# A fused attention and two-layer feed-forward kernel: four times the tolerance for weight steps between the attention's fixed steps

## The chip, the core and the metric

One core of one Trainium2 chip runs the whole program in one launch. The metric is the device time of that launch in microseconds, the median of three timed runs: 1220.61 us for the kernel before (1220.47 to 1222.97). Differences below about 0.2% (2.4 us) are not told from no change here.

## What is computed

Attention over 4 batches, 12 heads, 448 positions and head size 64, with a root-mean-square norm on q and k, followed by two feed-forward layers over 1792 tokens, 768 wide with 2048 hidden units. The weights come as 64-bit floats. In short:

```
q_n, k_n = rmsnorm(q, g_q), rmsnorm(k, g_k)
scores = (q_n @ k_n.T) / sqrt(64);  attn = softmax(scores);  x = attn @ v        # 4 x 12 heads
h = x @ w_in;   x = (h * sigmoid(h)) @ w_out                                     # moe_
h = x @ w_in2;  out = relu(h)**2 @ w_out2                                        # moe2_
```

## The kernel before

Every product is made of three matmuls in a reduced 32-bit form, with each operand split into an upper and a lower part.

**Attention** works on 24 pairs of heads, 0 to 23. For one pair, DMAs load q and k (line 516) and v (633). ScalarE squares them (527), VectorE sums (536), GpSimd and VectorE run Newton steps for the inverse root (544 to 580) and scale (589), and TensorE transposes the scaled q and k (601) into the tile T (610 to 619). Four chunks of 112 rows follow: scores (654) on TensorE, the row maximum on VectorE (665), the exponential on ScalarE (672), which also adds up its row sums into the tile `sum`, a transpose of E on TensorE (681), and a copy of that by VectorE or ScalarE (481, 483) into PT. Two rounds of products with v (730) end the pair. VectorE then inverts the row sums (701, 702). These 112 x 8 numbers must be laid along the other axis, so they go to DRAM by one DMA, `rd<-sum` (709), and come back spread over partitions by two, `R<-rd` (718). GpSimd multiplies the pair's result by R (753). For the first 12 pairs the result is split into the tile xb for the first layer; for the others it is stored by `x<-xf` (785).

`sum` has three buffers. The first exponential of pair p+3 therefore waits until the DMA `rd<-sum` of pair p has landed. `R` has two buffers, the tiles with q and k three.

**Weights** are made from 64-bit words by steps on a whole unit (768 numbers a partition for w_in, 512 for w_out). A unit is loaded as `raw` (846, two buffers). ScalarE takes the magnitude (853), VectorE clamps (857), shifts (861), puts the sign in (867) and the low bits in (873). The result, W, is stored by a DMA for later use (`ki` or `ko`, 881) and split into the upper part (493 or 495) and the lower part (502). I number the units 0, 1, 2, ... in order of use: 0 to 3 are the first of w_in, 4 to 9 the first of w_out.

**Layer 1** runs `up` (954, 18 matmuls each) and `down` (1008). `up` ends in tanh (966) and a product (971) into one of four tiles `g`, and from there in two parts into `gg`. The memory of `gg` belongs to a second pool, which takes the place of the attention's tiles. So the first write of `gg` waits until all of the attention has been done, the last store `x<-xf` included. **Layer 2** follows (1170 to 1273).

**The order** on every engine comes from a planner in the kernel that runs at build time, and each engine takes its instructions strictly in that order. Nearly all DMAs are issued by SyncE (SP), also in order: an issue that waits for data holds back all issues behind it. Every step of the attention has a hand-written place in a table (`nominal`), and each engine takes its attention steps in the order of that table. All other steps, the weights' above all, fill the gaps. The planner's rule for this is in `forward`, line 211: a step without a place may go ahead of the next attention step of its engine only if it ends, by the planner's own durations, at most FIT after the time at which that attention step could start:

```
nx = max(f, ready[next.n][e]) if not left[next.n] else max(f, next.nom + late)
if st + steps[n].on[e][0] > nx + FIT:
    continue
```

FIT is set on line 39.

Of the kernel before, what the change touches and what calls it, by code (L numbers as in the profile page):

```python
# [35 lines left out]

T2 = 5.3
EVEN, ODD = 0.0, 3.67
FIT = 0.1

# [54 lines left out]
class Plan:  # L97
# [81 lines left out]
    def forward(self, due):  # L179
# [16 lines left out]
        while len(order) < len(steps):  # L196
            best = None
            for e in ENGINES:
                f = free[e]
                next = fixed[e][-1] if fixed[e] else None  # L200
                for n in wait[e]:
# [7 lines left out]
                    if next is not None and steps[n] is not next:  # L209
# [3 lines that stand above are left out]
# [1129 lines left out]
```

## Time and profile before

| | |
|---|---|
| timed runs, median | 1220.61 us |
| profiled execution, its own time | 1222.14 us |
| its span | 1220.2 us |
| TensorE matmul busy | 1187.6 us (97%) |
| VectorE busy | 917.9 us (75%) |
| ScalarE busy | 547.2 us (45%) |
| GpSimd busy | 248.9 us (20%) |
| DMA queue of SP, share of 16 engines | 60.9% |

The attention fills the first 296 us, the first layer reaches to about 760 us, and the second layer the rest. TensorE is nearly always busy, so what a change in one stage is worth shows where TensorE waits, and in what would make it wait. In the profile's rows a time is counted from the span's start. A number in brackets with an arrow is the time for which the engine sat idle before the row, and what ended that.

### The profile page before, as it was taken

What the parts mean: (1) busy time and instruction counts of PE and PEld (TensorE: products, weight loads), DVE (VectorE), ACT (ScalarE), POOL (GpSimd) and SP (SyncE); (2) the same over time, 40 slices, a digit from 0 to 9 for tenths busy, and PEclk for the clock granted to TensorE, in tenths of its full rate; (3) what the DMA queues carried; (4) which work ended last, traced back from release to release, by engine and by line L of the source; (5) the groups of instructions that cost most, each with busy time, mean ns of one, the idle gap of its engine ahead of it and who ended that gap; (6) DMA issues with size and microseconds to landing.
All of it is one profiled execution on the core that took longest, in us unless ns stands there. A gap on an engine that the chain in (4) does not pass through costs nothing.

```text
span 1220.2 us, 19070 instructions
## 1 busy us (share of the span) xinstructions
PE 1187.6 (97%) x6960; PEld 1045.2 (86%) x6960; DVE 917.9 (75%) x1596; ACT 547.2 (45%) x1141; POOL 248.9 (20%) x459
## 2 busy tenths in 40 slices
PE   4999999998899999999999999999999999999998
PEld 3666666666799999998999998899999999999998
DVE  6988888887789886879798968866667973555554
ACT  6889888874334232424332315343333434211111
POOL 5466666531000000112010001011111130000000
PEclk9999999999899999999999999999999999999999
DMA  5456555548676645596888756946655785444444
GB/s 165 77 71 89 86 73 97 91 68 148 174 230 186 177 135 177 171 353 203 253 250 266 230 165 219 390 162 237 221 194 204 268 312 199 166 158 143 143 148 137
DMA packets 134109, 220.75 MB, mean 181 GB/s; under 512 B 31104, under 2 KB 99456, under 8 KB 134016
## 3 DMA queue, kind: packets, MB, share of 16 engines
q1 hardware_dynamic: 134016, 219.54, 60.9%
q8 instruction: 55, 0.90, 0.3%
q14 instruction: 38, 0.31, 0.2%
HBM read 145.88 MB, written 73.62 MB: 180 GB/s over the span
## 4 chain that ended last, share of the span: by engine, by line
PE 87%; DMA 6%; DVE 4%; ACT 1%; issue 1%; POOL 1%; SPq 0%; ACTq 0%; DVEq 0%
PE s L1008 18%; PE s L1246 17%; PE t L954 17%; PE t L1170 11%; PE t L681 6%; PE pv L730 6%; PE s L654 6%; PE pv L1170 4%; PE t L601 2%; DMA yf<-y 2%; DMA raw<-in_moe_w_out_dram 1%; DMA raw<-in_moe_w_in_dram 1%; DMA rd<-sum 1%; DMA w<-su 1%; DMA su<-w 1%
## 5 line engine op out<-in xcount | busy, mean ns | idle before, releaser
L954 PE MATMUL t<-xb,w 128*128 128x448 f32 x1152 | 242.2, 368 | 6.7 <-DVE g L971 6.7
L1008 PE MATMUL s<-gg,w 128*128 128x448 f32 x1152 | 239.5, 365 | 0.8 <-DVE g L1020 0.8
L954 PEld LDWEIGHTS t<-xb,w 128*128 128x128 f32 x1152 | 217.6, 189 | 25.9 <-DVE g L971 8.1
L1008 PEld LDWEIGHTS s<-gg,w 128*128 128x128 f32 x1152 | 216.2, 188 | 18.6 <-DVE g L1020 1.1
L1246 PE MATMUL s<-w,gh 128*128 128x384 f32 x896 | 227.6, 334 | 0.1
L1246 PEld LDWEIGHTS s<-w,gh 128*128 128x128 f32 x896 | 162.0, 188 | 1.5 <-DMA w<-su 0.4
L1273 DVE TENSOR_TENSOR gg<-s,gg 128x384 f32<-128x384 f32 x196 | 107.7, 554 | 61.5 <-PE s L1246 61.2
L1246 PE MATMUL s<-w,gl 128*128 128x384 f32 x448 | 149.7, 334 | 0.0
L672 ACT ACTIVATE E<-s,mx 112x448 f32<-112x448 f32 x192 | 121.2, 645 | 17.5 <-DVE mx L665 17.3
L1186 DVE TENSOR_TENSOR g<-t,g 128x448 f32<-128x448 f32 x96 | 58.4, 620 | 81.3 <-ACT g L481 57.0
L665 DVE TENSOR_REDUCE mx<-s 112x1 f32<-112x448 f32 x192 | 110.8, 619 | 10.3 <-PE s L654 8.0
L681 PEld LDWEIGHTS t<-ident,E 112*112 112x112 f32 x768 | 74.3, 135 | 37.5 <-ACT E L672 19.3
L681 PE MATMUL t<-ident,E 112*112 112x112 f32 x768 | 96.1, 268 | 4.8 <-ACT E L672 4.1
L654 PE MATMUL s<-T 64*112 64x448 f32 x576 | 85.5, 402 | 3.0 <-ACT T L610 3.0
L502 DVE TENSOR_TENSOR w<-W,w 128x768 fp32r<-128x768 f32 (+1 forms) x97 | 83.8, 871 | 3.1 <-ACT w L493 2.4
L1246 PEld LDWEIGHTS s<-w,gl 128*128 128x128 f32 x448 | 84.1, 188 | 0.0
L730 PE MATMUL pv<-PT,vv 112*64 112x224 f32 x768 | 83.3, 359 | 0.0
L502 POOL TENSOR_TENSOR w<-W,w 128x512 fp32r<-128x512 f32 (+1 forms) x15 | 24.1, 1604 | 279.2 <-ACT w L493 207.4
L493 ACT CAST w<-W 128x768 fp32r<-128x768 f32 (+1 forms) x64 | 47.9, 751 | 72.0 <-PE s L1008 45.7
L1196 ACT ACTIVATE g<-g 128x448 f32<-128x448 f32 x48 | 27.5, 576 | 97.3 <-DVE g L1186 96.7
L502 POOL TENSOR_TENSOR gl<-g,gh 128x448 fp32r<-128x448 f32 x12 | 14.7, 1223 | 266.2 <-DVE gh L495 198.9
L730 PEld LDWEIGHTS pv<-PT,vv 112*64 112x64 f32 x768 | 51.4, 136 | 20.0 <-issue 0.9
(109 smaller groups left out, 1754.0 us busy)
## 6 DMA issues: line engine op xcount, KB each, us to landing
raw<-in_moe_w_in_dram SPq DMA_DIRECT2D x32, 768.0 KB, 5.4
raw<-in_moe_w_out_dram SPq DMA_DIRECT2D x24, 512.0 KB, 4.4
raw<-in_moe_w_out_dram SPq DMA_DIRECT2D x16, 768.0 KB, 6.3
su<-w SPq DMA_DIRECT2D x16, 768.0 KB, 7.1
w<-su SPq DMA_DIRECT2D x16, 768.0 KB, 5.5
yf<-y SPq DMA_DIRECT2D x48, 224.0 KB, 4.1
ki<-W SPq DMA_DIRECT2D x16, 384.0 KB, 5.8
ko<-W SPq DMA_DIRECT2D x24, 256.0 KB, 4.3
```

The costliest lines, as they stand in the source:

```text
L502: kind, when, any_t(n, rate), lambda e: engine(e).tensor_tensor(o(), a(), h(), ALU.subtract),
L654: nc.tensor.matmul(pts[j].ap[:CP, :S], T.ap[r, 0, a, c * CP:(c + 1) * CP], T.ap[r, 1, b_], start=(k_ == 0), stop=(k_ == 2),)
L665: lambda e, pt=pt, mx=mx: nc.vector.tensor_reduce(mx.ap, pt.ap[:CP, :S], AX.X, ALU.max, negate=True),
L672: lambda e, j=j, c=c, pt=pt, mx=mx, E=E: nc.scalar.activation(E.ap[:, j], pt.ap[:CP, :S], AF.Exp, bias=mx.ap, accum_out=sums.ap[:, j, c:c ...
L681: nc.tensor.transpose(pe.ap[:CP, m * CP:(m + 1) * CP], E.ap[:, j, m * CP:(m + 1) * CP], ident.ap)
L730: nc.tensor.matmul(pv.ap[j * D:(j + 1) * D, c2 * CT * CP:(c2 + 1) * CT * CP], vr.ap[:, j * NCH + m, :], pt.ap[:, j * NCH + m].rearrange("p ...
L954: nc.tensor.matmul(pt.ap[:, :S], w_()[:, c, :], x[c // HC].ap[:, a, c % HC, :], start=(c == 0 and n == 0), stop=(c == NC6 - 1 and n == 2),)
L1008: nc.tensor.matmul(pt.ap[:, :S], w_()[:, f, :], gg.ap[:, k, a, f, :], start=(f == 0 and n == 0), stop=(f == HQ - 1 and n == 2),)
L1170: nc.tensor.matmul(pt.ap[:, :S], w_()[:, c0 + c, :], view(b, a, c)(), start=(start and c == 0 and k == 0), stop=(c == HC - 1 and k == 2), ...
L1186: lambda e: nc.vector.tensor_tensor(o.ap, pt.ap[:, :S], a.ap, ALU.add),
L1246: nc.tensor.matmul(pt.ap[:, :NH], g.ap[:, fi, tc_ * P:(tc_ + 1) * P], w_()[:, 0, nh * NH:(nh + 1) * NH], start=(n == 0), stop=(n == 5),)
L1273: lambda e, o=o, pt=pt: nc.vector.tensor_tensor(o(), pt.ap[:, :NH], o(), ALU.add),
```

## The change

One number: steps that have no place in the attention's table may end up to 0.4 instead of 0.1 after the time at which the next attention step could start.

```
 T2 = 5.3
 EVEN, ODD = 0.0, 3.67
-FIT = 0.1
+FIT = 0.4
```

No instruction's work changes. The orders of VectorE, ScalarE, GpSimd and SP change from the start of the attention to the start of layer 1; a few weight steps go to another of the engines that may take them. TensorE's order stays, apart from three matmuls of the first `up` that move over one group of products with v.

**SP, pair 6.** The two DMAs `R<-rd` bring back the sums of pair 5, `rd<-sum` stores those of pair 6, `vv` and `qk` are loads of v, q and k for later pairs. Before:

```order
L718 DMA R_1547<-rd_1406 64x448 x2
L709 DMA rd_1594<-sum_1307 112x8x1
L633 DMA vv_1606<-in_v_dram 112x2x256
L516 DMA qk_1702<-in_q_dram 112x2x256
L516 DMA qk_1702<-in_k_dram 112x2x256
L718 DMA R_1734<-rd_1594 64x448 x2
```

And now:

```order
L718 DMA R_1591<-rd_1451 64x448 x2
L846 DMA raw_1625<-in_moe_w_out_dram 128x4x256
L881 DMA ki2_1627<-W_614 128x768
L709 DMA rd_1641<-sum_1329 112x8x1
L633 DMA vv_1644<-in_v_dram 112x2x256
L516 DMA qk_1754<-in_q_dram 112x2x256
L516 DMA qk_1754<-in_k_dram 112x2x256
L718 DMA R_1810<-rd_1641 64x448 x2
```

The load of unit 4 and the store of unit 2 now stand between the two DMAs of pair 5 and the store of pair 6's sums. Such a piece stands at the same place ahead of the stores of pairs 3, 6, 9, 11, 12 and 14 (loads of units 3 to 8). The load of unit 9 stands ahead of the two DMAs of pair 14, and that of unit 2 behind the store of pair 0. Before, units 0 and 1 are loaded at the very start and the next load, of unit 2, comes behind the store of pair 20; now none is left between pair 15 and the end of the attention.

**VectorE, end of pair 6**: the last part of a later T (617), the inverse of the sums (701, 702) and two Newton steps (551, 558). Before:

```order
L617 SCALAR_TENSOR_TENSOR T_1491<-t_1561,G_134,T_1491 128x448
L701 TENSOR_SCALAR sum_1307<-sum_1307 112x8
L702 RECIPROCAL sum_1307<-sum_1307 112x8
L551 TENSOR_SCALAR ib_1592<-ms_1500 112x16
L558 TENSOR_SCALAR y_1596<-ib_1592 112x16
```

And now:

```order
L873 SCALAR_TENSOR_TENSOR W_614<-raw_503,W_614 128x768
L617 SCALAR_TENSOR_TENSOR T_1515<-t_1583,G_136,T_1515 128x448
L701 TENSOR_SCALAR sum_1329<-sum_1329 112x8
L702 RECIPROCAL sum_1329<-sum_1329 112x8
L551 TENSOR_SCALAR ib_1637<-ms_1530 112x16
L495 CAST w_1639<-W_614 128x768
L558 TENSOR_SCALAR y_1646<-ib_1637 112x16
```

The low bits and the upper part of unit 2 have moved in.

**ScalarE, from the last chunk of pair 22 to the start of pair 23** (`sum_4270` and `sum_4429` before, `sum_4356` and `sum_4504` now). Before:

```order
L481 COPY xf_4382<-pv_4256 128x448
L853 ACTIVATE W_4384<-raw_4286 128x768
L672 ACTIVATE E_4400,sum_4270<-s_4373,mx_4391 112x448
L672 ACTIVATE E_4400,sum_4270<-s_4374,mx_4398 112x448
L481 COPY PT_4410<-t_4393 112x4x112
L672 ACTIVATE E_4428,sum_4429<-s_4402,mx_4423 112x448
```

And now:

```order
L481 COPY xf_4460<-pv_4342 128x448
L672 ACTIVATE E_4476,sum_4356<-s_4451,mx_4467 112x448
L672 ACTIVATE E_4476,sum_4356<-s_4452,mx_4474 112x448
L481 COPY PT_4486<-t_4469 112x4x112
L672 ACTIVATE E_4503,sum_4504<-s_4478,mx_4498 112x448
```

The magnitude of unit 2 (853) no longer stands ahead of these exponentials; it now stands in pair 1, ahead of the exponentials there.

## Rows read from the trace of the kernel before

**Rows 1.** Busy time by stretch, four attention laps together (the last line's sum).

```profile
sum 45.00, PE 45.00 PEld 31.03 DVE 39.26 ACT 40.14 POOL 29.01; mean PE 11.25 PEld 7.76 DVE 9.81 ACT 10.04 POOL 7.25
```

**Rows 2.** The chain that ended last: start us, us, what.

```profile
107.49 1.66 PE pv L730 x16
...
118.71 1.67 PE pv L730 x16
...
364.03 27.36 PE t L954 x135
```

**Rows 3.** Timeline of TensorE, end of attention: start us, us, engine line op.

```profile
275.19 1.73 PE L730 MATMUL pv<-PT,vv 112*64 112x224 f32 x16
280.11 1.21 PE L681 MATMUL t<-ident,E 112*112 112x112 f32 x8 [3.19 <-ACT E L672]
...
285.27 1.74 PE L730 MATMUL pv<-PT,vv 112*64 112x224 f32 x16
...
295.58 16.42 PE L954 MATMUL t<-xb,w 128*128 128x448 f32 x78
317.96 15.06 PE L954 MATMUL t<-xb,w 128*128 128x448 f32 x63 [5.96 <-DVE g L971]
332.86 12.32 PE L1008 MATMUL s<-gg,w 128*128 128x448 f32 x60
```

**Rows 4.** Timeline of ScalarE, end of attention and start of layer 1.

```profile
278.56 0.89 ACT L853 ACTIVATE W<-raw 128x768 f32<-128x768 f32 x1 [5.17 <-DMA raw<-in_moe_w_in_dram]
...
322.39 1.50 ACT L493 CAST gg<-g 128x448 fp32r<-128x448 f32 x3 [0.53 <-DMA x<-xf]
```

**Rows 5.** Busy time by stretch, 300 to 350 us; the clock stands behind POOL.

```profile
300.00:350.00 50.00, 44.04 (x206) 39.99 (x205) 37.88 (x65) 18.26 (x31) 2.85 (x2) 0.93 0.75 192
```

**Rows 6.** Timeline of SP's DMA issues, pairs 6 to 8.

```profile
115.14 1.09 SPq L718 DMA_DIRECT2D R<-rd  x2
116.34 0.52 SPq L709 DMA_DIRECT2D rd<-sum  x1
...
127.12 0.52 SPq L709 DMA_DIRECT2D rd<-sum  x1
```

**Rows 7.** Line 709 (`rd<-sum`), 90 to 270 us, 16 issues.

```profile
DMA to landing us min/median/max: 9.4/9.5/11.5
```

**Rows 8.** Timeline of ScalarE, first exponentials of pairs 9 and 22.

```profile
119.29 0.67 ACT L672 ACTIVATE E<-s,mx 112x448 f32<-112x448 f32 x1
...
265.15 0.67 ACT L672 ACTIVATE E<-s,mx 112x448 f32<-112x448 f32 x1
```

**Rows 9.** Timeline of SP's DMA issues, pairs 19 to 23.

```profile
263.61 1.25 SPq L718 DMA_DIRECT2D R<-rd  x2
...
266.83 0.40 SPq L846 DMA_DIRECT2D raw<-in_moe_w_in_dram  x1
...
274.24 1.09 SPq L718 DMA_DIRECT2D R<-rd  x2
275.44 0.52 SPq L709 DMA_DIRECT2D rd<-sum  x1
...
287.89 1.09 SPq L718 DMA_DIRECT2D R<-rd  x2
...
300.22 0.53 SPq L709 DMA_DIRECT2D rd<-sum  x1
...
311.88 1.09 SPq L718 DMA_DIRECT2D R<-rd  x2
```

**Rows 10.** The page's DMA issues: count, KB each, median us to landing.

```profile
raw<-in_moe_w_in_dram SPq DMA_DIRECT2D x32, 768.0 KB, 5.4
raw<-in_moe_w_out_dram SPq DMA_DIRECT2D x24, 512.0 KB, 4.4
```

**Rows 11.** The page's groups: busy us, mean ns of one, idle before.

```profile
L502 DVE TENSOR_TENSOR w<-W,w 128x768 fp32r<-128x768 f32 (+1 forms) x97 | 83.8, 871 | 3.1 <-ACT w L493 2.4
```

## Prediction, made before the changed kernel ran

> **What bounds the kernel now.** I read the attention first, since only its orders change. In four laps of it TensorE is busy for all of 45.00 us; VectorE has 39.26 and ScalarE 40.14 [rows 1]. So a lap is TensorE's, and by the chain of work that ended last it takes 118.71 - 107.49 = 11.22 us [rows 2]. VectorE has (45.00 - 39.26) / 45.00 x 11.22 = 1.43 us of it free.
>
> At the attention's end TensorE does wait. After the products at 275.19 it sits idle for 3.19 us, and the next such group starts at 285.27, 10.08 us later, where half a lap would be 5.61 [rows 3]. ScalarE stood for 5.17 us before the magnitude of unit 2, whose load landed only then, with the exponentials queued behind it [rows 4]. The second wait is 5.96 us long, ahead of 317.96 [rows 3]. The 63 matmuls after it took 15.06 us; at the 27.36 us for 135 of a calm stretch [rows 2] they would have taken 12.77. The granted clock of that stretch was 0.93 on average [rows 5], a part of it at the lower level of 1.2 GHz. The two losses there are 5.96 + 2.3 = 8.3 us.
>
> The third thing to see is not a wait of TensorE, but it sits close behind. SP issues the two DMAs that bring back pair 6's sums at 115.14, pair 7's store at 116.34 and pair 8's at 127.12 [rows 6]. The store takes 9.4 to 11.5 us to land, mostly 9.5 [rows 7], and SP waits for that before it issues the two DMAs, then the next store. This chain takes 127.12 - 116.34 = 10.78 us a lap against TensorE's 11.22: it has 0.44 us to spare. And someone waits for it. The first exponential of pair p+3 needs pair p's `sum` buffer back. Pair 6's store has landed at 115.14 and pair 9's exponential starts at 119.29: 4.15 us [rows 6, 8]. For pairs 19 and 22 it is 263.61 and 265.15: 1.54 us [rows 8, 9].
>
> **The change part by part.** The weight steps move forward in a body: ten units instead of two are loaded before pair 16, eight of them are worked through there, and eight stores go with them.
>
> A, removed: the wait of ScalarE at 278.56. No load or magnitude of a weight is left there. Gain 10.08 - 5.61 = 4.5 us.
>
> C, added: seven laps in which a load of a unit, mostly with a store of another, stands ahead of a store of sums. The trace of before shows two laps in which a load and a weight store were still draining as the sums' store was issued. The first, with 768 KB, is 275.44 to 287.89, 12.45 us; the second, with 512 KB, is 300.22 to 311.88, 11.66 us [rows 9]. Against 9.5 these are 2.95 and 2.16 us more. One unit of 768 KB (unit 3) and six of 512 KB give 2.95 + 6 x 2.16 = 15.9 us. In those two laps part of the load had gone before, so this leans low. For the other end I take the whole transfer: 768 KB land 1.0 us after 512 KB would [rows 10], hence 4 us per MB, 3.1 and 2.1 us, and a weight store of half that size half as much again: 4.6 + 6 x 3.1 = 23 us. I keep 15.9, the lengths of real laps. A reason that excludes a gain here: nothing that the chain carries is taken away before pair 20. Of the 15.9 the slack absorbs what is left of it at the end, 1.5 us [rows 8, 9]; the 0.44 us a lap were used up in the kernel before, else that slack would not have shrunk from 4.15. So ScalarE's exponentials, and TensorE with them, come 14.4 us later by pair 23.
>
> The Trainium skill says of such queues (DMA: Bandwidth & Descriptors, Queues, rings and completion order) that each DMA engine takes descriptors in ring order and that a semaphore counts up only after every earlier write of that engine. By that rule the weights ahead of the sums' store must be through first; the two long laps agree with it.
>
> D, added: unit 2's load stands behind pair 0's store, as in the lap of 266.83, where it took 278.56 - 266.83 = 11.7 us until ScalarE had it [rows 4, 9]. Its magnitude stands ahead of pair 1's exponentials. At most the 4.5 us of A, at least 0 if ScalarE comes to it late enough; I take 2.
>
> E, VectorE: units 0 to 7 bring about 17 more steps of 768 and 18 of 512 numbers into the attention. A long one takes 0.87 us [rows 11]; the clamps, shifts and casts are shorter, and I put the sum at 20 to 24 us. In the 16 laps from pair 3 to pair 19 there are 16 x 1.43 = 23 us free, and C stretches these laps by 14 more. I cost E at nothing for that; without that cover it is 0 to 2 us. GpSimd, which gets two lower parts, has 16 of 45 us free [rows 1]. The pushed attention steps themselves are late by under a microsecond, and the row maxima catch up in the next gap.
>
> B, the start of layer 1. Weights no longer hold TensorE at 317.96. What is late next is the store of pair 23's result, which opens the memory of `gg`. The return DMAs of pair 20 move from 274.24 [rows 9] to 274.2 + 15.9 + 2 = 292.1; three laps of 10.78 later those of pair 23 go, at 324.4. Before, from there to the first write of `gg` it took 322.39 - 311.88 = 10.5 us [rows 4, 9], with two weight loads in the queue; I take 9: 333.4. TensorE ends the attention at 295.6 - 4.5 + 14.4 + 2 = 307.5, can do seven `up` without `gg` (four tiles `g`, three PSUM buffers), 7 x 18 x 0.2027 = 25.5 us, and stands at 333.0. It then waits for one tile `g` to be handed on, four short steps, about 2.5 us, and the eighth `up` of 3.65 ends at 339.6. In the kernel before, `down` starts at 332.86 [rows 3]. So +6.7 us; with a drop of the clock after the wait, as after the 3.19 us, up to +8.4. I take +7.5.
>
> After that TensorE is as full as before, and the shift stays. Profiled 1222.1 + 7.5 = 1229.6; the median of the timed runs is 1.5 us below the profiled time, so **1228.1 us**.
>
> **The rivals.** *The return chain has room after all* (the other side). It decides at pair 6: if its store still lands by 119.3, C falls away. Then A gives 4.5, the start of layer 1 all of its 8.3, D costs 2 and E 1: -9.8 us, 1210.8. For it speaks that the store of the sums is only 3.5 KB. Against it speaks that this store takes 9.5 us in every lap, and more in both laps with weights in front. The Trainium skill's fit (DMA: Bandwidth & Descriptors, Anatomy of one DMA) of 2.0 us plus bytes by 436 KB per us would make that store an estimated 2 us; with it the chain would have 7 us to spare, and this rival would hold. The trace says 9.5.
>
> *The gains and the chain cancel.* If half of each load slips into the time in which the sums' store waits for DRAM, C is 8 - 1.5 = 6.5, TensorE ends the attention at about 299.6, `gg` opens at 325.5, seven `up` end at 325.1 and the eighth at 331.7: -1.2 us, 1219.4.
>
> *The whole transfer counts*, 23 us. Then the attention ends 7.1 us later than in the forecast and so does everything behind it: 1235.2; if TensorE's waits of 2 us or so also bring the clock down, some more. No row shows the clock fall after a wait that short.
>
> *The change doesn't do what it says*: excluded by the order, in which the steps have moved.
>
> **How the numbers follow.** Forecast 0.58 (own range 1223.5 to 1234); whole transfer 0.12; cancel 0.14; room 0.16. Faster by over 0.2% (2.4 us, about what a measurement tells from no change) is the rival with room: 0.16. Within it: 0.14. Slower: 0.70. The range 1213 to 1237 leaves out most of the case with room and the far end of the dear one.
>
> **What would show it.** Issues of `rd<-sum` about 11 us apart in plain laps and 13 or more with a load in front; ScalarE's first exponential of a pair waiting for a DMA from pair 9 on; no wait near 276; the attention's end near 307, the first write of `gg` near 333, `down` near 340. I am wrong if ScalarE never waits for the sums' store, or if laps with weights stay at 11.2 us.

## The result, and the profile after

The changed kernel takes **1237.45 us** (median; 1231.96 to 1243.06) against 1221.79 of the kernel before on the same chip. The ratio is 1.0124, with a 95% interval of 1.0087 to 1.0161: slower by 1.2%. On the 1220.61 us that the prediction started from, that is 1235.7. The forecast had 1228.1 and a range of 1213 to 1237, so the sign was right and the loss of 15 us was twice the 7.5 foreseen. The profiled execution took 1240.2 us, its span is 1238.4, 18.2 us longer than before. Two executions of the experiments below, one of e2 (1766.16 us) and the profiled one of e5 (2966.65 us), ran in a slower state of the chip and are left out of the ratios.

Where the time went shows in TensorE's timeline. In each row: start, length, engine, line, operation; in brackets the idle time before and what ended it. `L730` are the products of a pair, `L681` the transposes of E.

```profile
46.48 1.73 PE L730 MATMUL pv<-PT,vv 112*64 112x224 f32 x16
51.99 0.60 PE L681 MATMUL t<-ident,E 112*112 112x112 f32 x4 [3.78 <-ACT E L672]
...
59.36 3.25 PE L730 MATMUL pv<-PT,vv 112*64 112x224 f32 x16
...
203.14 2.04 PE L681 MATMUL t<-ident,E 112*112 112x112 f32 x8 [6.41 <-ACT E L672]
...
314.21 22.77 PE L954 MATMUL t<-xb,w 128*128 128x448 f32 x111
345.46 7.67 PE L954 MATMUL t<-xb,w 128*128 128x448 f32 x27 [8.48 <-DVE g L971]
352.97 3.20 PE L1008 MATMUL s<-gg,w 128*128 128x448 f32 x15
```

The wait at the end of the attention is gone (the 3.19 us of [rows 3]), but there are two new and longer ones, in pair 1 and in pair 13. Behind each the matmuls are slow for a while: the products at 59.36 take 3.25 us where others take 1.73. The granted clock says why (stretch, busy times, clock behind POOL):

```profile
50.00:60.00 10.00, 7.57 (x36) 5.08 (x38) 6.64 (x15) 8.00 (x21) 4.14 (x14) 0.64 0.37 81
...
200.00:210.00 10.00, 6.82 (x32) 4.60 (x32) 4.32 (x12) 8.22 (x21) 4.12 (x15) 0.51 0.46 68
```

A mean of 0.64 and of 0.51 is for most of these stretches the lower level of 1.2 GHz. Layer 1's first long run of `up` starts at 314.21 instead of 295.58 [rows 3], 18.6 us later, and its first `down` at 352.97 instead of 332.86, 20.1 us later.

ScalarE's timeline tells who held TensorE up:

```profile
50.44 0.89 ACT L853 ACTIVATE W<-raw 128x768 f32<-128x768 f32 x1 [6.06 <-DMA raw<-in_moe_w_in_dram]
51.22 0.63 ACT L672 ACTIVATE E<-s,mx 112x448 f32<-112x448 f32 x1
...
200.83 0.66 ACT L853 ACTIVATE W<-raw 128x512 f32<-128x512 f32 x1 [8.49 <-DMA raw<-in_moe_w_out_dram]
...
342.05 1.50 ACT L493 CAST gg<-g 128x448 fp32r<-128x448 f32 x3 [12.29 <-DMA raw<-in_moe_w_in_dram]
```

The first two waits are those of a **magnitude**, of unit 2 and of unit 7, that stands until its load is there, with the exponentials queued behind it. (The third row is the first write of `gg`, to which I come back under B.) It is the wait that stood at 278.56 before [rows 4], now twice and in the middle of the attention. What the forecast had counted on, an exponential that waits for the store of the sums, does not occur. These are ScalarE's two longest waits in total from 60 to 300 us (total, times, longest), and line 672, the exponentials, waits for row maxima alone:

```profile
ACT E L672 <- DVE mx L665: 14.3, 20, 1.4
ACT W L853 <- DMA raw<-in_moe_w_out_dram: 14.1, 4, 8.5
```

SP's issues around the two loads:

```profile
37.19 0.32 SPq L709 DMA_DIRECT2D rd<-sum  x1
37.60 0.50 SPq L633 DMA_DIRECT2D vv<-in_v_dram  x1
38.27 0.39 SPq L846 DMA_DIRECT2D raw<-in_moe_w_in_dram  x1
...
175.76 0.53 SPq L846 DMA_DIRECT2D raw<-in_moe_w_out_dram  x1
...
188.29 1.09 SPq L718 DMA_DIRECT2D R<-rd  x2
189.47 0.54 SPq L846 DMA_DIRECT2D raw<-in_moe_w_out_dram  x1
190.06 0.50 SPq L881 DMA_DIRECT2D ko<-W  x1
190.66 0.38 SPq L709 DMA_DIRECT2D rd<-sum  x1
```

Unit 2's load is issued 1.1 us behind a store of sums and is ready 50.44 - 38.27 = 12.2 us later; unit 7's goes 1.2 us ahead of one and is ready after 11.4 us. Units 4 to 6, whose loads also go 1.2 us ahead of such a store, took 7.4, 6.2 and 6.2 us by the same reckoning, with waits of 1.6 to 2.1 us.

### The profile page after: what moved, and what is told of

The parts are those of the page before. It is cut to its first block, busy times and chain, and to the rows that moved or that the text cites. A ratio compares the mean times of both kernels' runs of the same rounds, so it can differ in the third digit from the quotient of the medians.

```text
span 1238.4 us, 19057 instructions
## 1 busy us (share of the span) xinstructions
PE 1195.7 (97%) x6960; PEld 1048.9 (85%) x6960; DVE 913.2 (74%) x1602; ACT 543.0 (44%) x1136; POOL 257.7 (21%) x458
## 3 DMA queue, kind: packets, MB, share of 16 engines
q1 hardware_dynamic: 134016, 219.54, 60.4%
## 4 chain that ended last, share of the span: by engine, by line
PE 80%; DMA 8%; DVE 4%; POOL 3%; ACT 3%; issue 1%; SPq 0%; POOLq 0%; ACTq 0%; DVEq 0%
PE s L1008 19%; PE t L954 17%; PE s L1246 17%; PE t L1170 11%; PE pv L1170 4%; PE t L681 4%; PE pv L730 3%; PE s L654 3%; DMA raw<-in_moe_w_out_dram 3%; DMA rd<-sum 2%; DMA raw<-in_moe_w_in_dram 1%; ACT E L672 1%; PE t L601 1%; DMA yf<-y 1%; DMA w<-su 1%
## 5 line engine op out<-in xcount | busy, mean ns | idle before, releaser
L672 ACT ACTIVATE E<-s,mx 112x448 f32<-112x448 f32 x192 | 121.2, 645 | 18.3 <-DVE mx L665 17.8
L681 PEld LDWEIGHTS t<-ident,E 112*112 112x112 f32 x768 | 76.1, 137 | 49.7 <-ACT E L672 24.9
L681 PE MATMUL t<-ident,E 112*112 112x112 f32 x768 | 100.6, 273 | 14.0 <-ACT E L672 10.9
L730 PE MATMUL pv<-PT,vv 112*64 112x224 f32 x768 | 84.8, 363 | 0.0
L493 ACT CAST w<-W 128x768 fp32r<-128x768 f32 (+1 forms) x59 | 44.2, 753 | 65.8 <-PE s L1008 43.5
L966 ACT ACTIVATE g<-t 128x448 f32<-128x448 f32 x64 | 34.5, 543 | 82.8 <-PE t L954 82.3
```

What stands on the lines that cost most here:

```text
L672: lambda e, j=j, c=c, pt=pt, mx=mx, E=E: nc.scalar.activation(E.ap[:, j], pt.ap[:CP, :S], AF.Exp, bias=mx.ap, accum_out=sums.ap[:, j, c:c ...
L681: nc.tensor.transpose(pe.ap[:CP, m * CP:(m + 1) * CP], E.ap[:, j, m * CP:(m + 1) * CP], ident.ap)
L730: nc.tensor.matmul(pv.ap[j * D:(j + 1) * D, c2 * CT * CP:(c2 + 1) * CT * CP], vr.ap[:, j * NCH + m, :], pt.ap[:, j * NCH + m].rearrange("p ...
```

## The experiments

Three theories stood. **Theory 1** is the forecast's: the sums' store holds back the exponentials. **Theory 2**: magnitudes that now stand ahead of exponentials wait for raw loads, and these land late because the store of the sums, 896 pieces of 4 bytes, drains at the same time. **Theory 3**: VectorE has too much to do. To compare the kernels I use the starts of the products with v in TensorE's timeline, one profiled execution of each kernel. The table gives, in us, the start of the first pair's, the time from one named pair's to another's, and the start of pair 23's. In e6 and e7 the profiled execution was the longest of ten, 6.6 and 9.2 us above the median:

| kernel | first | 1 to 3 | 3 to 13 | 13 to 14 | 22 to 23 | pair 23 |
|---|---|---|---|---|---|---|
| before | 28.86 | 22.4 | 112.2 | 11.2 | 14.4 | 289.55 |
| after | 29.66 | 31.4 | 117.1 | 20.8 | 9.4 | 308.74 |
| e1, fourth `sum` | 29.75 | 29.5 | 116.2 | 16.4 | 9.4 | 301.71 |
| e2, 16 bytes, after | 29.76 | 22.4 | 115.8 | 12.0 | 9.4 | 290.04 |
| e3, 16 bytes, before | 28.67 | 22.4 | 112.2 | 11.2 | 9.4 | 284.34 |
| e4, late loads, all | 28.60 | 22.4 | 112.4 | 12.1 | 9.4 | 285.68 |
| e6, late loads, attention | 30.02 | 22.4 | 117.4 | 12.4 | 9.4 | 293.71 |
| e7, VectorE alone | 30.24 | 22.4 | 113.5 | 16.5 | 9.4 | 292.52 |
| e8, VectorE alone, 16 bytes | 29.71 | 22.4 | 114.0 | 12.1 | 9.3 | 288.32 |
| e9, unit 2 later | 29.82 | 22.4 | 122.3 | 11.3 | 9.4 | 302.09 |
| e10, tolerance 0.6, 16 bytes | 30.51 | 22.4 | 118.0 | 11.2 | 9.4 | 291.91 |

**e1: a fourth buffer for the sums.**

```
-        sums = sa([CP, 2, NCH], F32, "sum", 3)
+        sums = sa([CP, 2, NCH], F32, "sum", 4)
```

> The kernel after with a fourth buffer for the tile `sum`; the order on every engine stays as it was. Theory 1 (the forecast's: the first exponential of pair p+3 waits for the store of pair p's sums) expects the laps with a load in front to stop costing: up to 14 us back, about 1224. Theory 2 (ScalarE stands at the magnitudes of units 2 to 7, whose loads land 11 to 12 us after their issue because the sums' store is draining at the same time) expects no change, 1237 within 2.5 us, with the waits of about 6 us at 50 and 8.5 us at 201 still there. Theory 3 (VectorE has too much work in the laps) expects no change either.

Measured: 1232.19 us against 1217.43 of before, 1.0122 (1.0089 to 1.0155), the ratio of the kernel after. Both waits are there:

```profile
50.45 0.89 ACT L853 ACTIVATE W<-raw 128x768 f32<-128x768 f32 x1 [5.99 <-DMA raw<-in_moe_w_in_dram]
...
194.69 0.66 ACT L853 ACTIVATE W<-raw 128x512 f32<-128x512 f32 x1 [5.06 <-DMA raw<-in_moe_w_out_dram]
```

The second is shorter, and pair 23 starts 7 us earlier than in the profile of after. Whether that is the buffer or the spread from run to run, the next run was to say.

**e5: the kernel after once more.**

> The kernel after, unchanged, beside the next three on the same chip, so that the laps and the time of the fourth `sum` buffer can be set beside it. If that buffer gave something back after all, this time stands above 1.0122 of before by more than 0.004, and its lap with unit 7's magnitude (20.8 us before, 16.4 with the fourth buffer) stays near 20; if the difference is the spread from run to run, it falls between 1.008 and 1.016.

Measured: 1230.53 us, 1.0091 (1.0061 to 1.0121). There is no profile of it to set beside that of e1, so on the lap it says nothing. With three buffers the kernel after reaches the time of e1, so the fourth gives nothing that these runs can tell, and not the 14 us of theory 1. Theory 1 falls.

**e2 and e3: the sums stored in pieces of 16 bytes**, in the kernel after and in the kernel before. The result is the same; GpSimd's product reads R with a stride and takes 1.37 instead of 1.15 us.

```
-        rd = dram([2, NCH, CP], "rd", 3)
+        rd = dram([2, CP, NCH], "rd", 3)
-                rd.ap.rearrange("j c p -> p (j c)"), sums.ap.rearrange("p j c -> p (j c)")),
+                rd.ap.rearrange("j p c -> p j c"), sums.ap),
-                    rd.ap[j].rearrange("c p -> (c p)").unsqueeze(0).to_broadcast([D, S])),
+                    rd.ap[j].rearrange("p c -> (p c)").unsqueeze(0).to_broadcast([D, S])),
-            lambda e: engine(e).tensor_tensor(t.ap, t.ap, R.ap, ALU.mult),
+            lambda e: engine(e).tensor_tensor(t.ap.rearrange("d (c p) -> d c p", p=CP),
+                t.ap.rearrange("d (c p) -> d c p", p=CP), R.ap.rearrange("d (p c) -> d c p", c=NCH), ALU.mult),
```

> The kernel after with the sums stored in DRAM as [head, row, chunk] instead of [head, chunk, row]: one DMA of 224 pieces of 16 bytes instead of 896 of 4 bytes; GpSimd's product reads R with a stride of four numbers. Every engine's order stays. Theory 2 expects the store to land in 3 to 5 us instead of 9.5, the raw loads issued beside it in 6 to 8 us instead of 11 to 12, ScalarE's waits of 6.06 and 8.49 us at the magnitudes of units 2 and 7 to shrink to under 2 us, and 10 to 18 us back: 1219 to 1227. Theory 1 expects the same sign, since the store leaves the chain too, but then the laps of pairs 3 to 13 (117.1 us now) to fall by their 4.9 us; by theory 2 alone about half of that. Theory 3 expects the loss of about 0.5 us a lap in pairs 3 to 13 to stay. If GpSimd's strided read costs, its product gets longer than the present one, which is off TensorE's path.

> The kernel before with the same 16-byte layout of the stored sums, every engine's order as before. If the 4-byte store is what delays raw loads, ScalarE's wait of 5.17 us at 278.56 shrinks to under 1 us and the start of layer 1 comes earlier: 4 to 10 us faster than before (1212 to 1218). If the loads are late for another reason, 1221 as before.

Measured: the kernel after falls to 1212.23 us, 0.9964 (0.9939 to 0.9988) of the kernel before; the kernel before falls to 1207.38, 0.9916 (0.9883 to 0.9949). Line 709 from issue to landing, 90 to 270 us, in the kernel after:

```profile
DMA to landing us min/median/max: 7.9/9.1/10.4
```

and in e2:

```profile
DMA to landing us min/median/max: 1.5/3.0/4.4
```

The same two magnitudes in e2, with every engine's order as in the kernel after:

```profile
44.75 0.91 ACT L853 ACTIVATE W<-raw 128x768 f32<-128x768 f32 x1 [0.26 <-DMA raw<-in_moe_w_in_dram]
...
182.04 0.71 ACT L853 ACTIVATE W<-raw 128x512 f32<-128x512 f32 x1
```

Unit 2's load, issued at 38.36, is now ready after 6.4 us instead of 12.2. Laps 1 to 3 are back at 22.4 us and lap 13 falls from 20.8 to 12.0: these two places were 18.6 us of the loss, and 17.8 of them are gone. Between the two kernels no order and no amount of data differs, only the pieces and GpSimd's read of them (the queue's packets fall from 134016 to 117888, as 24 stores of 224 pieces instead of 896 would have it). So it is the 4-byte store that makes the loads late, and the late loads that cost. In e3 the wait of 278.56 [rows 4] is gone as well (14.4 to 9.4 in the last lap), and `down` starts at 318.04. It beats both kernels. Both runs gained more than was expected, because the return of pair 23's sums is shorter too: from its products to the first write of `gg` it takes 23.6 us in e2 and 24.0 in e3 against 33.3 in the kernel after and 32.8 before, and TensorE's wait ahead of the last `up` is gone. One part came out otherwise: pairs 3 to 13 fall only from 117.1 to 115.8 us, where theory 2 asked for half of the 4.9 us. Most of that loss is not the late loads. The first write of `gg` in e2:

```profile
313.69 1.51 ACT L493 CAST gg<-g 128x448 fp32r<-128x448 f32 x3 [2.63 <-DMA x<-xf]
```

The Trainium skill (DMA: Bandwidth & Descriptors, Rules for kernel authors) says that a last dimension with a stride becomes one descriptor per element and should be made contiguous; with a quarter of the pieces the same 3.5 KB land in a third of the time (3.0 against 9.1 us), which agrees.

Left in e2 against e3 are 4.8 us, in the start and in laps 3 to 14.

**e4 and e6: the planner told that raw loads land later**, in the whole program (e4), and for those issued before 296 us alone (e6).

```
-        self.extra = 4.5 if kind == "store_r" else 0.0
+        self.extra = 4.5 if kind == "store_r" else 6.0 if kind == "load_raw" else 0.0
```

```
-                end = dma + s.extra
+                end = dma + (6.0 if s.kind == "load_raw" and st < 296 else s.extra)
```

> The kernel after with one number of the planner changed: it takes the raw loads to land 6 us later than it thought, so that magnitudes stand 12 to 18 us behind their loads in ScalarE's order. Weights still go into the attention (fewer of them), and loads still stand ahead of the sums' stores. Theory 2 expects the waits at magnitudes gone and 10 us or more of the 15 back: 1220 to 1227, pairs 1 to 2 and 13 to 14 at about 11.2 us a lap. Theory 1 expects the long laps, so 1232 or more. Theory 3 expects laps of 11.5 to 11.8 us where VectorE works weights.

> The kernel after, with the planner taking raw loads to land 6 us later than it thought, but only for loads that it issues before 296 us, so that layer 1 is planned as in the kernel after. Weights still enter the attention. Theory 2 (magnitudes waiting for late raw loads) expects ScalarE's waits at magnitudes under 1 us in the attention, the products of pair 23 near 286 (308.7 in the kernel after), layer 1's first `down` near 328, and 1212 to 1224. What is left against the kernel before is then VectorE's part. If it stays above 1230, late raw loads are not the cause.

Measured: e4 takes 1251.93 us, 1.0285 (1.0248 to 1.0323), a miss, though its attention is what theory 2 expected: 22.4 us for laps 1 to 3, pair 23 at 285.68. The loss is in layer 1, where TensorE waits for weights (waits of TensorE: total, times, longest):

```profile
PE s L1008 <- ACT w L493: 7.4, 2, 4.3
PE t L954 <- DVE w L495: 3.7, 1, 3.7
PE s L1008 <- DVE w L495: 3.4, 2, 1.8
```

The edit was too wide: it also put the magnitudes of layer 1 farther behind their loads, and only two `raw` exist. (It also enters the planner's pass from the end backwards, which e6 leaves as it was.) e6 leaves the loads of layer 1 alone and takes 1221.11 us, 1.0018 (0.9992 to 1.0044): of a loss of 0.9 to 1.2% next to nothing is left. In its profile pair 23 starts at 293.71, not near 286 as expected. One long lap is the largest part of that, and there ScalarE waits for a load of q, not for weights; since this execution was the longest of ten, the lap may be its own:

```profile
70.87 0.63 ACT L527 ACTIVATE sq<-qk 112x512 f32<-112x512 f32 x1 [4.36 <-DMA qk<-in_q_dram]
```

**e7 and e8: the wider tolerance on VectorE alone**, with the old layout (e7) and with 16 bytes (e8).

```
-                        if st + steps[n].on[e][0] > nx + FIT:
+                        if st + steps[n].on[e][0] > nx + (FIT if e == "dve" else 0.1):
```

> The kernel after with the wider tolerance on VectorE alone; on ScalarE, GpSimd and SP it is 0.1 as before. Units still go into the attention, but ScalarE takes their magnitudes only in gaps, mostly 12 to 17 us after the load, units 4 and 5 after 7. Theory 2 expects waits only at units 4 and 5, 2 to 4 us each: 3 to 8 us of loss in the attention against the kernel before, 1216 to 1226. Theory 3 (VectorE's work itself stretches the laps) expects laps of 11.4 us and more all through pairs 4 to 14, as in the kernel after where no magnitude waits (12.3, 12.2, 11.8), and 1224 to 1232.

> The same (wider tolerance on VectorE alone) with the 16-byte layout of the sums, so that no raw load is late. With that layout the kernel after takes 1212.2 and the kernel before 1207.4; the 4.8 us between them lie in the start (1.1) and in laps 5 to 14 (4.8 together). If VectorE's pushed steps cost these, they stay: 1211 to 1213. If ScalarE's pushed steps (magnitudes and upper parts ahead of exponentials) cost them, they go: 1207 to 1208.5.

Measured: e7 takes 1217.92 us, 0.9989 (0.9962 to 1.0017), no change from before. With weights in the attention but magnitudes in gaps, the change costs nothing on balance. Of the two magnitudes that were expected to wait, unit 4's does not and unit 5's does, for 5.21 us at 186.05; it is the 16.5 of lap 13. The wider tolerance on ScalarE alone leaves every engine's order as it was before. So the loss takes both parts: VectorE's lets the units in, ScalarE's puts their magnitudes ahead of exponentials, by the planner 6 to 7 us after the load was issued.

e8 takes 1210.22 us, between its two expectations. Pair 23 starts 4.0 us later than in e3, in e2 5.7. So of the 5.7 us about 4 come with VectorE's tolerance and 1.7 with ScalarE's; the timed medians split 4.8 into 2.8 and 2.0. The ratios, 0.9916 (e3), 0.9936 (e8, 0.9909 to 0.9964) and 0.9964 (e2), have intervals that overlap from one to the next, so this split is rough.

**e9: only unit 2's magnitude later.**

```
-                end = dma + s.extra
+                end = dma + (6.0 if s.kind == "load_raw" and 30 < st < 45 else s.extra)
```

> The kernel after, with the planner taking the one load that it issues between 30 and 45 us (unit 2) to land 6 us later; all other loads as before. Unit 2's magnitude moves 11 us back, and the units behind it are shifted by some 12 us but keep their magnitudes 6 to 7 us behind their loads. Theory 2 expects the wait of 6 us in pair 1 to go (laps 1 and 2 together 22.4 instead of 31.4: 9 us back), and the waits of the later units to stay, one of them large if the sums' store is issued within about 1 us of the load, as for unit 7 now: 1219 to 1226. If pair 1's wait is not what cost those 9 us, 1230 stays.

Measured: the 9.0 us of laps 1 to 3 go as expected, but the time stays: 1230.78 us, 1.014 (1.0089 to 1.019). Unit 3 has taken unit 2's place. Its load, in the shifted order, is issued 1.2 us behind a store of sums (82.59 and 83.77 on SP) and is ready 14.3 us later:

```profile
98.03 0.89 ACT L853 ACTIVATE W<-raw 128x768 f32<-128x768 f32 x1 [8.63 <-DMA raw<-in_moe_w_in_dram]
```

Unit 7's magnitude also still waits, now in the lap from pair 14 to 15, which takes 17.7 instead of 11.2 us, so that the table's lap 13 to 14 looks clean:

```profile
205.69 0.66 ACT L853 ACTIVATE W<-raw 128x512 f32<-128x512 f32 x1 [5.64 <-DMA raw<-in_moe_w_out_dram]
```

Taking one wait away moved it. Of what was tried, only taking away what makes the loads late, or keeping all magnitudes farther behind them, helped.

**e10: tolerance 0.6 with 16 bytes.** The edit is that of e3 and `FIT = 0.6`.

> The kernel before with 16-byte sums and a tolerance of 0.6 instead of 0.1 on all engines: nine units are loaded before 132 us, the magnitudes 6 to 12 us behind their loads. With 0.1 it takes 1207.4, with 0.4 1212.2. If what is left is the attention's steps being pushed late by weight steps on VectorE and ScalarE, the cost grows with the tolerance, since each push may be half as long again: laps of 12 us and more between pairs 1 and 11, 1213 to 1219. If it is a matter of how many weight steps lie in the attention, their number is the same and so is the time, 1211 to 1213.

Measured: 1215.11 us, 0.9983 (0.9963 to 1.0003). From 0.1 over 0.4 to 0.6 the times are 1207.4, 1212.2 and 1215.1: without late loads the cost still grows with the tolerance, clearly from 0.1 to 0.6 (0.9916 to 0.9983); the second step alone lies within the intervals. In part it comes in small pieces, as TensorE's waits of the whole run show (in e3 this row has 0.2 us, in e2 1.7):

```profile
PE t L681 <- ACT PT L481: 3.6, 8, 0.8
```

## Why the prediction was right in sign and short in size

**A**, the wait at 278.56: right. It is gone, and the last lap falls from 14.4 to 9.4 us (5.0, forecast 4.5).

**C**, 14.4 us through the sums' buffer: wrong, and it carried the forecast. The seven stores with a load in front did take longer, 10.1 to 14.3 us from their issue to that of the DMAs that bring the sums back, together 18.6 us above 9.5 (forecast 15.9). But ScalarE never stood at an exponential for it, which the forecast had named as its sign of being wrong, and a fourth buffer changed nothing. The failing step was to let seven longer laps add up against a slack of 1.5 us as if TensorE's own laps stayed at 11.22. The other stores from pair 1 to pair 13 took 7.4 to 9.4 us, but for one of 11.4, so the long ones did not add up, and TensorE's laps were stretched by something else. It was close once: pair 6's store had landed by 131.06, and pair 9's first exponential started at 131.62. The rows that C was priced from also held more than a load in front: in the kernel before, further loads were issued behind those two stores, at 277.34 and at 301.40 and 305.04. The 2 us that the forecast set beside the 9.5 came from a fit of the Trainium skill (DMA: Bandwidth & Descriptors, Anatomy of one DMA) that is given there for DMAs issued by GpSimd; this store is issued by SP, so the fit says little of it.

**D**, the magnitude of unit 2: the right mechanism, mis-sized, and counted once. I bounded it at 4.5 and took 2. It measured 9.0 (31.4 against 22.4): the wait of TensorE of 3.78 us and, behind it, slow matmuls at the lower clock, which the bound had left out. The row that I used for it, 11.7 us from issue to ScalarE behind a store of sums, is right: 12.2 here, 14.3 in e9. What I did not do was ask the same of the other units. Unit 7's magnitude cost 9.6 more, and the magnitudes of units 4 to 6 smaller waits.

**E**, VectorE at nothing, 0 to 2: too low. Pairs 3 to 13 took 4.9 us more, the start 0.8. With 16 bytes, where no load is late, VectorE's tolerance cost about 4 us (e8), the whole change 5.7 (e2). Free time on an engine averaged over a lap does not mean that a pushed step of the attention costs nothing. In e7 no net loss is left of it; there the 5 us of A are gained as well.

**B**, the start of layer 1: the chain as described, at later times. The return DMAs of pair 23 were issued at 331.46 (forecast 324.4), and the first write of `gg` followed 10.6 us behind (forecast 9, before 10.5). TensorE stood from 336.98, after all the `up` that it could do without `gg`, to 345.46, and the clock took some of the `up` behind. But this only hands on what the attention lost: pair 23 is 19.2 us late and `down` 20.1.

**The sum** by the runs: 0.8 for the start, 9.0 for unit 2, 4.9 for pairs 3 to 13, 9.6 for unit 7, less 5.0 of A make 19.3 at pair 23, of which 18.2 are left in the span. The forecast's 11.9 for the attention came mostly from a term that the runs do not show. That the time still fell within the range, near its upper end, was luck: late loads that it had counted once, at 2 us, cost 18.6. The rival *the whole transfer counts* was nearest in time (1235.2) and as wrong in mechanism, since it too went through the sums' buffer. The rival *the return chain has room after all* was nearer to the mechanism: C did fall away. Its time of 1210.8 assumed D at 2.

Still open is why unit 7's load, issued 1.2 us ahead of a store like those of units 4 to 6, took 11.4 us (8.7 in e1, 8.5 in e9) where theirs took 6.2 to 7.4. In all three traces it follows another unit's load by less than 14 us (189.47 and 175.76 above), those of units 4 to 6 by 23 us or more. No run varied that alone. Nor was it tried to issue the loads on another queue.

## What to carry to other kernels

When a rule lets steps move ahead of a critical engine's work, list every moved step that waits for a DMA, and compare its distance from the issue, in the new order, with the longest landing seen in the trace, not the median. Price such a wait by the idle time of TensorE plus the slow matmuls behind it. A small store with a stride can be the cause of late large loads: change its layout before its place.

## What the runs showed of the hardware that I had not expected

A store of 3.5 KB delays other transfers by more than its size says. Cut into 224 pieces of 16 bytes instead of 896 of 4, it landed in 3.0 instead of 9.1 us, and a load of 768 KB issued 1.1 us behind it was ready after 6.4 instead of 12.2 us.

The forecast said that no row shows the clock fall after a wait of 2 us or so. In e6 TensorE waited for 2.38 us before 73.41 and for 0.44 us more soon after, and in that stretch the granted clock was 0.83 on average; the transposes at 76.07 took 1.74 us for eight, where eight take 0.98 otherwise:

```profile
73.41 0.59 PE L681 MATMUL t<-ident,E 112*112 112x112 f32 x4 [2.38 <-ACT E L672]
74.45 0.60 PE L681 MATMUL t<-ident,E 112*112 112x112 f32 x4 [0.44 <-ACT PT L481]
...
76.07 1.74 PE L681 MATMUL t<-ident,E 112*112 112x112 f32 x8
```

```profile
70.00:80.00 10.00, 7.18 (x50) 4.65 (x48) 6.23 (x14) 8.69 (x22) 4.26 (x14) 0.83 0.45 78
```
